# A fused attention, mixer and feed-forward kernel: weight conversion moved between slots, a rounding moved from VectorE to ScalarE, and folds put in another order

## The chip, the cores and the metric

One core of a Trainium2 chip runs the whole program. The metric is the device time of one execution in microseconds; before and after are each given as the median of several executions, and one more execution is run under the profiler.

## The reference, cut to what is computed

```python
attn = A @ Z @ C @ v                      # landmark attention per head, Z by six Newton steps
x1 = moe(attn):   u = x + (x^T U V)^T;    x1 = u + relu(u @ w11) @ w12
X = np.fft.fft(np.fft.fft(x1, axis=1), axis=2)
u = x1 + np.real(X)
mu = np.mean(u, axis=-1, keepdims=True)
var = np.mean((u - mu) ** 2, axis=-1, keepdims=True)
un = (u - mu) / np.sqrt(var + 1e-06)
out = u + np.maximum(un @ w21, 0.0) @ w22
```

There are 8 batches of 576 tokens with 512 features; the hidden width of both feed-forward parts is 2048. The inputs are float32 and the weights float64.

## The kernel before, in words

Every operand of a matmul is held as two parts, a high part rounded to the matmul's format (fp32r) and a low part that holds the rest. A product of two such pairs takes three matmuls. The helper `split` (L49) makes a pair: ScalarE copies the value into the high part (L51), and VectorE or GpSimd subtracts it to get the low part (L52).

The float64 weights are converted on the chip. One piece (128 rows by 512 values) passes through `convert` (L90): `TENSOR_SCALAR`, `SCALAR_TENSOR_TENSOR`, `TENSOR_SCALAR`, `SCALAR_TENSOR_TENSOR`, `TENSOR_TENSOR` and one more `SCALAR_TENSOR_TENSOR` on VectorE (L96 to L106), an absolute value on ScalarE (L101), and the split into the tile `stg` on ScalarE and GpSimd. The result goes to DRAM with a DMA of 512 KB. There is one `stg` buffer, so the next split waits until that DMA has landed, and two buffers `wraw` for the float64 pieces.

The feed-forward work is a stream of slots. A slot is 12 matmuls of 128x512. In a first-layer slot, `up` (L318) then takes the bank from PSUM: ScalarE makes the high part with a Relu (L329), VectorE the low part (L330). There are 3 banks for it. In a second-layer slot pair, VectorE adds the former sum (L387), or ScalarE copies the bank (L385). The stage that matters here is the loop at L1582: 144 slots of the second pass and 96 of the third. Into it are laid, slot by slot, the instructions of eight `Mixer` objects (L1139), one for each batch, which compute the Fourier mixing and the normalisation. A mixer starts every 25 slots, from slot 33 on (L1577). Its list `steps` (L1339) is a table of numbers: (slot, step). The order in which a slot is written is: the stream's instructions, then the mixers' steps, then the conversion. All engines work their instructions in that order.

The mixer's steps that matter:

- `fold_d`, `fold_t`, `fold_2` (L1171 to L1186): VectorE folds the batch's data into an even part "e" and an odd part "o". `fold_split` (L1187) copies the high part on ScalarE (`he`, `ho`), `fold_low` (L1193) subtracts the low part on VectorE (`le`, `lo`). `over_d` (L1219) multiplies them with a table, from slot 10 of the mixer (even) and 13 (odd) on.
- `sums` (L1288), called by `sum_u` and `sum_sq` for each half n of the tokens, adds the four blocks of 128 features. It makes a pair in the tiles `he`, `ho`, `le`, `lo` again (four VectorE instructions, L1291 to L1294). `mean` (L1296) multiplies the pair with a matrix of 1/512. `centre` (L1305) subtracts the mean, ScalarE squares the result (L1314), `deviation` (L1317) calls `mean` a second time.
- The conversion runs as a generator. `Pace.step(n)` (L1468) takes up to n of its pieces in a slot; at the end of a weight piece it stops until the next slot. `BUSY` (L1580) names the mixer's slots in which nothing is converted.

```python
later = Pace(chained([staging_pairs(cv, 2), staging_sums(cv), staging_blocks(cv)]))
BUSY = (0, 1, *range(4, 9), 21, 22)
later.step(0 if s > 33 and (s - 33) % 25 in BUSY else 2)
```

Slot numbers of 25 and more of one mixer are the slots 0, 1, 2 and so on of the next one. In what follows the mixers are counted from the first to the eighth.

Of the kernel before, what the change touches and what calls it, by code (L numbers as in the profile page):

```python
# [15 lines left out]
ALU = mybir.AluOpType  # L16
# [18 lines left out]
def f32(ap):  # L35
    return ap.bitcast(F32)
# [3 lines left out]
def body(ctx: ExitStack, tc: tile.TileContext, qT, kT, vn, mU, mV, w11, w12, w21, w22,  # L40
         ident, bones, istack, tabs, out):
    nc = tc.nc
# [1096 lines left out]
    class Mixer:  # L1139
# [148 lines left out]
        def sums(self, n, x, nm):  # L1288
            a = self.fp.tile([P, 2, 290], F32, name="cc", bufs=2)[:, :, 0:HS]
            s = self.half[n]["s"] = self.fp.tile([P, 2, NF], F32R, name=nm + "eo"[n], bufs=1)[:, :, 0:HS]  # L1290
            nc.vector.tensor_tensor(a, x[:, 0:2], x[:, 2:4], op=ALU.add)  # L1291
            nc.vector.tensor_tensor(s[:, 0, :], a[:, 0, :], a[:, 1, :], op=ALU.add)
            nc.vector.tensor_tensor(a[:, 0, :], a[:, 0, :], f32(s[:, 0, :]), op=ALU.subtract)
            nc.vector.tensor_tensor(s[:, 1, :], a[:, 0, :], a[:, 1, :], op=ALU.add)  # L1294

        def mean(self, n):  # L1296
            ps = self.bank("l")[:, 0:HS]
# [39 lines left out]
            nc.sync.dma_start(rs[self.b][:, self.cols(n)], self.half[n]["r"])  # L1337

        def steps(self):  # L1339
            yield from ((0, self.load), (2, self.load_first), (3, self.fold_x), (4, self.sum_row), (5, self.row_high), (5, lambda: self.fold_d("e")),  # L1340
                        (5, lambda: self.fold_t("e")), (6, lambda: self.fold_d("o")), (6, lambda: self.fold_2("e")),
                        (7, self.fold_row), (7, lambda: self.fold_t("o")), (8, lambda: self.fold_split("e")),
                        (8, self.row_low), (8, lambda: self.fold_2("o")), (9, lambda: self.fold_low("e")),
                        (9, lambda: self.fold_split("o")), (10, lambda: self.fold_low("o")),
                        (11, self.load_rows))
            yield from ((s, lambda nm=nm, i=i: self.over_d(nm, i)) for s, nm, i in
                        ((10, "e", 0), (11, "e", 1), (12, "e", 2), (13, "o", 0), (14, "o", 1), (14, "o", 2)))
            yield from ((15, self.top_row), (16, lambda: self.odd(0)), (17, lambda: self.even(0)),
                        (18, lambda: self.unfold(0)), (18, lambda: self.unfold(3)), (18, lambda: self.odd(1)),
                        (19, lambda: self.even(1)), (20, lambda: self.unfold(1)), (20, lambda: self.unfold(2)),  # L1350
                        (21, self.store))
            for n in range(2):
                yield from ((21 + n, lambda n=n: self.sum_u(n)), (24 + n, lambda n=n: self.centre(n)),
                            (25 + n, lambda n=n: self.sum_sq(n)), (28 + n, lambda n=n: self.deviation(n)),
                            (26 + n, lambda n=n: self.put(n)), (29 + n, lambda n=n: self.newton(n)),
                            (30 + n, lambda n=n: self.put_scale(n)))

# [122 lines left out]
    with pool("mm") as mp, pool("pm", space=PSUM) as pm:  # L1480
# [91 lines left out]
        with tc.manual_schedule(), pool("cv") as cv:  # L1572
            with pool("fp") as fp, pool("fc") as fc, pool("pf", space=PSUM) as psb:
                f = {}
                slots = Slots()
                for b in range(B):
                    slots.add(33 + 25 * b, Mixer(fp, psb, f, b).steps())  # L1577
                later = Pace(chained([staging_pairs(cv, 2), staging_sums(cv), staging_blocks(cv)]))
                gen = mlp.stream(1)
                BUSY = (0, 1, *range(4, 9), 21, 22)  # L1580
                setup = fourier_setup(f, fc, fp)
                for s in range(N + 96):  # L1582
                    if s == N:
                        some(gen, 9)
                        gen = mlp.stream(2)
                    next(gen)
                    slots.run(s)
                    next(setup, 0)
                    later.step(0 if s > 33 and (s - 33) % 25 in BUSY else 2)
            assert not slots.at  # L1590
            chunks = [(0,)] + [(c, c + 1) for c in range(1, NCH, 2)]
            kinds = [(chunks[-1:], None, ByChunk(y2), quarter[0], None),
                     (chunks[-1:], ByChunk(y2), ByChunk(y2), quarter[1], None),
                     (chunks, ByChunk(y2), ByChunk(y3), staged[3][0:11], None),
                     (chunks, ByChunk(y3), Y, staged[3][11:22], (Scales(rs), U2))]
            with pool("tl") as mlp.last_pool, pool("tp", space=PSUM) as mlp.last_ps:
                last = mlp.quarters(UN, kinds, lambda s: s % 2 and later.step(2))
                next(last)
                for s in range(STEPS):
                    next(gen)  # L1600
                    next(last)
                    later.step(0 if s > 6 else 1)
                some(gen, 9)
                for _ in last:
                    pass
                later.rest()
# [83 lines left out]
```

## Time and profile before

| | |
|---|---|
| median of 3 runs | 1818.57 us (1816.17 to 1820.9) |
| profiled execution, its own time | 1816.94 us |
| its span, first to last instruction | 1815.2 us |
| TensorE matmul (PE) busy | 1786.8 us, 98% |
| VectorE (DVE) busy | 1117.6 us, 62% |
| ScalarE (ACT) busy | 734.9 us, 40% |
| GpSimd (POOL) busy | 274.5 us, 15% |
| DMA, mean rate | 182 GB/s |
| mean granted TensorE clock | 0.998 |

The busy share of an engine is an average over stages. The end of a matmul in the trace is modelled, so that a busy TensorE says little; the views that tell of the stage are the waits of TensorE, the chain of work that ended last and the instructions in order of time.

### The profile page before, as it was taken

Reading aid. Unit: us, or ns where it says so; the run is one execution under the profiler, and the core shown is the slowest. Engines: PE = TensorE matmul, PEld = TensorE weight load, DVE = VectorE, ACT = ScalarE, POOL = GpSimd, SP = SyncE. Lnnn points to the kernel's source line nnn. Section 1 sums busy time; section 2 is a strip of 40 time slices with the busy share of each in tenths; the row PEclk is TensorE's granted clock in tenths of the full one; section 3 lists DMA queues with packets and bytes.
Section 4 is the critical chain, followed back from the end, with each engine's and each line's share of the span. In section 5 each row is a group of like instructions: output and inputs, shape, how many; then the busy total and the mean of one; then the engine's idle time right before and its main releaser. Section 6 shows DMA issues by size and latency. Waiting matters only on the chain.

```text
span 1815.2 us, 30889 instructions
## 1 busy us (share of the span) xinstructions
PE 1786.8 (98%) x12037; PEld 1456.7 (80%) x12037; DVE 1117.6 (62%) x1984; ACT 734.9 (40%) x1507; POOL 274.5 (15%) x278
## 2 busy tenths in 40 slices
PE   6999999999999999999999999999999999999998
PEld 4777777777888888888888888888788888888887
DVE  7896665665423666847666685756651465438874
ACT  4554444344212333323233243434333566545542
POOL 3324221221200321111112111111200000000000
PEclk9999999999999999999999999999999999999999
DMA  7555456542448654535445753424466745477765
GB/s 250 184 174 179 148 168 212 170 153 100 142 146 292 206 199 163 190 115 192 143 163 194 274 178 119 141 105 151 157 208 223 275 157 167 146 256 244 225 192 162
DMA packets 189238, 329.57 MB, mean 182 GB/s; under 512 B 28938, under 2 KB 101226, under 8 KB 189092
## 3 DMA queue, kind: packets, MB, share of 16 engines
q1 hardware_dynamic: 184484, 318.16, 52.5%
q10 hardware_dynamic: 4608, 9.44, 1.4%
q8 instruction: 94, 1.54, 0.3%
q14 instruction: 52, 0.43, 0.1%
HBM read 213.42 MB, written 113.51 MB: 180 GB/s over the span
## 4 chain that ended last, share of the span: by engine, by line
PE 85%; DVE 9%; DMA 2%; ACT 2%; issue 1%; POOL 0%; SPq 0%; DVEq 0%; ACTq 0%
PE ps L377 9%; PE ps L379 8%; PE ps L378 8%; PE ps L325 8%; PE ps L327 8%; PE ps L326 8%; PE ps L593 4%; PE ps L594 4%; PE ps L592 4%; PE ps L417 4%; PE ps L416 4%; PE ps L418 4%; PE ps_f L77 1%; PE ps_f L78 1%; PE ps_f L76 1%
## 5 line engine op out<-in xcount | busy, mean ns | idle before, releaser
L325 PE MATMUL ps<-x,w 128*128 128x512 f32 x800 | 317.8, 397 | 0.0
L377 PE MATMUL ps<-g,w 128*128 128x512 f32 x800 | 316.6, 396 | 0.0
L379 PE MATMUL ps<-g,w 128*128 128x512 f32 x800 | 312.1, 390 | 0.1
L327 PE MATMUL ps<-x,w 128*128 128x512 f32 x800 | 312.1, 390 | 0.0
L326 PE MATMUL ps<-x,w 128*128 128x512 f32 x800 | 311.8, 390 | 0.0
L378 PE MATMUL ps<-g,w 128*128 128x512 f32 x800 | 311.6, 390 | 0.0
L330 DVE SCALAR_TENSOR_TENSOR g<-ps,g 128x512 fp32r<-128x512 f32 x200 | 137.8, 689 | 234.0 <-ACT g L329 233.5
L329 ACT ACTIVATE g<-ps 128x512 fp32r<-128x512 f32 x200 | 119.0, 596 | 312.7 <-PE ps L327 312.2
L377 PEld LDWEIGHTS ps<-g,w 128*128 128x128 f32 x800 | 150.2, 188 | 33.3 <-issue 3.5
L379 PEld LDWEIGHTS ps<-g,w 128*128 128x128 f32 x800 | 150.1, 188 | 32.7 <-DVE g L330 0.5
L327 PEld LDWEIGHTS ps<-x,w 128*128 128x128 f32 x800 | 150.2, 188 | 32.5
L325 PEld LDWEIGHTS ps<-x,w 128*128 128x128 f32 x800 | 150.2, 188 | 30.5
L378 PEld LDWEIGHTS ps<-g,w 128*128 128x128 f32 x800 | 150.4, 188 | 28.5
L326 PEld LDWEIGHTS ps<-x,w 128*128 128x128 f32 x800 | 150.5, 188 | 28.2
L592 PE MATMUL ps<-g,w 128*128 128x512 f32 x352 | 136.9, 389 | 0.0
L593 PE MATMUL ps<-g,w 128*128 128x512 f32 x352 | 136.9, 389 | 0.0
L594 PE MATMUL ps<-g,w 128*128 128x512 f32 x352 | 136.9, 389 | 0.0
L387 DVE TENSOR_TENSOR xf<-ps,xf 128x512 f32<-128x512 f32 x76 | 52.2, 687 | 86.7 <-PE ps L379 85.0
L52 POOL TENSOR_TENSOR x<-xf,x 128x512 fp32r<-128x512 f32 (+7 forms) x50 | 62.5, 1252 | 206.6 <-ACT x L51 183.5
L416 PE MATMUL ps<-xs,w 128*128 128x512 f32 x208 | 80.9, 389 | 0.0
L417 PE MATMUL ps<-xs,w 128*128 128x512 f32 x208 | 80.9, 389 | 0.0
L418 PE MATMUL ps<-xs,w 128*128 128x512 f32 x208 | 80.9, 389 | 0.0
(388 smaller groups left out, 2999.5 us busy)
## 6 DMA issues: line engine op xcount, KB each, us to landing
w<-d SPq DMA_DIRECT2D x62, 512.0 KB
d<-stg SPq DMA_DIRECT2D x54, 512.0 KB
wraw<-w SPq DMA_DIRECT2D x48, 512.0 KB
res<-y SPq DMA_DIRECT2D x80, 256.0 KB
y<-xf SPq DMA_DIRECT2D x64, 256.0 KB
y<-out SPq DMA_DIRECT2D x52, 256.0 KB
xf<-y SPq DMA_DIRECT2D x40, 256.0 KB
u<-u1T ACTq DMA_DIRECT2D x32, 288.0 KB
```

The source lines that it names most:

```text
L325: nc.tensor.matmul(ps, wh, xh, start=k == 0, stop=False)
L326: nc.tensor.matmul(ps, wl, xh, start=False, stop=False)
L327: nc.tensor.matmul(ps, wh, xl, start=False, stop=k == 3)
L377: nc.tensor.matmul(ps, wh, gh, start=k == m0, stop=False)
L378: nc.tensor.matmul(ps, wl, gh, start=False, stop=False)
L379: nc.tensor.matmul(ps, wh, gl, start=False, stop=k == m1 - 1)
L416: nc.tensor.matmul(ps, wh, xh, start=first and k == 0, stop=False, skip_group_check=True)
L417: nc.tensor.matmul(ps, wl, xh, start=False, stop=False, skip_group_check=True)
L418: nc.tensor.matmul(ps, wh, xl, start=False, stop=last and k == 1, skip_group_check=True)
L592: nc.tensor.matmul(ps[j], wh, gh, start=first, stop=False, skip_group_check=True)
L593: nc.tensor.matmul(ps[j], wl, gh, start=False, stop=False, skip_group_check=True)
L594: nc.tensor.matmul(ps[j], wh, gl, start=False, stop=k == ks[3], skip_group_check=True)
```

## The change

Three things change. First, `sums` no longer writes the high part with an add. It adds the blocks in full float32, ScalarE copies (and so rounds) the result, and the low part is one subtraction in a new step `sums_low`, one slot after `sum_u` and two slots after `sum_sq`. Second, the folds are given other slots: the even part goes through to its low part at mixer slot 8 (it was 9), and the odd folds follow. Third, the conversion has no part in mixer slots 2 and 3 either, and in the slots that are left takes up to 3 pieces (it was 2); in the last stage it takes up to 2 in the first seven slots (it was 1).

```diff
             nc.vector.tensor_tensor(a, x[:, 0:2], x[:, 2:4], op=ALU.add)
-            nc.vector.tensor_tensor(s[:, 0, :], a[:, 0, :], a[:, 1, :], op=ALU.add)
-            nc.vector.tensor_tensor(a[:, 0, :], a[:, 0, :], f32(s[:, 0, :]), op=ALU.subtract)
-            nc.vector.tensor_tensor(s[:, 1, :], a[:, 0, :], a[:, 1, :], op=ALU.add)
+            nc.vector.tensor_tensor(a[:, 0, :], a[:, 0, :], a[:, 1, :], op=ALU.add)
+            self.half[n]["a"] = a[:, 0, :]
+            nc.scalar.copy(s[:, 0, :], a[:, 0, :])
+
+        def sums_low(self, n):
+            a, s = self.half[n]["a"], self.half[n]["s"]
+            nc.vector.tensor_tensor(s[:, 1, :], a, f32(s[:, 0, :]), op=ALU.subtract)
...
-                        (8, self.row_low), (8, lambda: self.fold_2("o")), (9, lambda: self.fold_low("e")),
+                        (8, lambda: self.fold_low("e")), (8, lambda: self.fold_t("o")),
...
-                yield from ((21 + n, lambda n=n: self.sum_u(n)), (24 + n, lambda n=n: self.centre(n)),
-                            (25 + n, lambda n=n: self.sum_sq(n)), (28 + n, lambda n=n: self.deviation(n)),
+                yield from ((21 + n, lambda n=n: self.sum_u(n)), (22 + n, lambda n=n: self.sums_low(n)), (24 + n, lambda n=n: self.centre(n)),
+                            (25 + n, lambda n=n: self.sum_sq(n)), (27 + n, lambda n=n: self.sums_low(n)), (28 + n, lambda n=n: self.deviation(n)),
...
-                BUSY = (0, 1, *range(4, 9), 21, 22)
+                BUSY = (*range(0, 9), 21, 22)
...
-                    later.step(0 if s > 33 and (s - 33) % 25 in BUSY else 2)
+                    later.step(0 if s > 33 and (s - 33) % 25 in BUSY else 3)
...
-                    later.step(0 if s > 6 else 1)
+                    later.step(0 if s > 6 else 2)
```

TensorE's instructions and their order are the same before and after. Three places where the order on the other engines differs:

VectorE, the folds of the third mixer, before (`big` holds a fold that is being made, `cc` its second step, `le` and `he` the even low and high parts):

```order
L1175 TENSOR_TENSOR big<-U 128x1152
L1179 TENSOR_TENSOR big<-big 128x2x287
L387 TENSOR_TENSOR xf<-ps,xf 128x512
L1175 TENSOR_TENSOR big<-U 128x1152
L1185 TENSOR_TENSOR cc<-big 128x289 x2
L52 TENSOR_TENSOR x<-xf,x 128x512
L1208 TENSOR_TENSOR cc<-X 1x289
L1179 TENSOR_TENSOR big<-big 128x2x287
L387 TENSOR_TENSOR xf<-ps,xf 128x512
L1216 TENSOR_TENSOR X<-X,row 1x289
L1185 TENSOR_TENSOR cc<-big 128x289 x2
L1195 TENSOR_TENSOR le<-cc,he 128x578
```

and now:

```order
L1175 TENSOR_TENSOR big<-U 128x1152
L1179 TENSOR_TENSOR big<-big 128x2x287
L387 TENSOR_TENSOR xf<-ps,xf 128x512
L1185 TENSOR_TENSOR cc<-big 128x289 x2
L1208 TENSOR_TENSOR cc<-X 1x289
L1216 TENSOR_TENSOR X<-X,row 1x289
L52 TENSOR_TENSOR x<-xf,x 128x512
L1175 TENSOR_TENSOR big<-U 128x1152
L387 TENSOR_TENSOR xf<-ps,xf 128x512
L1195 TENSOR_TENSOR le<-cc,he 128x578
L1179 TENSOR_TENSOR big<-big 128x2x287
L1185 TENSOR_TENSOR cc<-big 128x289 x2
```

The second and third odd folds now stand behind the even low part, not ahead of it.

VectorE, the sums of squares of the fourth mixer, before, from the first `centre` on (`Z<-U,ps_l`); `le` and `lo` are the pairs of the first and second half, and `g<-ps,g` is the stream's low part of a slot:

```order
L1309 TENSOR_TENSOR Z<-U,ps_l 128x1152
L330 SCALAR_TENSOR_TENSOR g<-ps,g 128x512
L1291 TENSOR_TENSOR cc<-big 128x2x288
L1292 TENSOR_TENSOR le<-cc 128x288
L1293 TENSOR_TENSOR cc<-cc,le 128x288
L1294 TENSOR_TENSOR le<-cc 128x288
L1309 TENSOR_TENSOR Z<-U,ps_l 128x1152
L330 SCALAR_TENSOR_TENSOR g<-ps,g 128x512
L1291 TENSOR_TENSOR cc<-big 128x2x288
L1292 TENSOR_TENSOR lo<-cc 128x288
L1293 TENSOR_TENSOR cc<-cc,lo 128x288
L1294 TENSOR_TENSOR lo<-cc 128x288
```

and now, from the last two conversion instructions on (three more stand ahead of them, behind the first `centre`; before, this place held none):

```order
L134 SCALAR_TENSOR_TENSOR cvp<-wraw,cvp 128x512
L135 TENSOR_TENSOR cvp<-cvp,cva 128x512
L330 SCALAR_TENSOR_TENSOR g<-ps,g 128x512
L1291 TENSOR_TENSOR cc<-big 128x2x288
L1292 TENSOR_TENSOR cc<-cc 128x288
L1313 TENSOR_TENSOR Z<-U,ps_l 128x1152
L330 SCALAR_TENSOR_TENSOR g<-ps,g 128x512
L1291 TENSOR_TENSOR cc<-big 128x2x288
L1292 TENSOR_TENSOR cc<-cc 128x288
L330 SCALAR_TENSOR_TENSOR g<-ps,g 128x512
L1298 TENSOR_TENSOR le<-cc,le 128x288
```

The pair of the first half, `le`, was complete ahead of the second `centre`; now it is complete only behind the second half's sums and behind the stream's low part of one more slot.

ScalarE at the same place, before (`big<-Z` is the square):

```order
L329 ACTIVATE g<-ps 128x512
L1314 ACTIVATE big<-Z 128x1152
L329 ACTIVATE g<-ps 128x512
L1314 ACTIVATE big<-Z 128x1152
L329 ACTIVATE g<-ps 128x512
L51 CAST x<-xf 128x512
```

and now:

```order
L132 ACTIVATE wraw<-wraw 128x512
L329 ACTIVATE g<-ps 128x512
L1318 ACTIVATE big<-Z 128x1152
L1294 CAST le<-cc 128x288
L329 ACTIVATE g<-ps 128x512
L1318 ACTIVATE big<-Z 128x1152
L1294 CAST lo<-cc 128x288
L329 ACTIVATE g<-ps 128x512
L51 CAST x<-xf 128x512
```

A copy of each half's high part now stands behind its square and ahead of the stream's next Relu.

## Rows read from the trace of the kernel before

**Rows 1.** Windows: stretch, length, then busy time (and count) by engine.

```profile
582.00:690.00 108.00, 108.00 (x478) 89.41 (x477) 76.41 (x116) 35.27 (x62) 28.56 (x23) 1.00 0.58 194
690.00:1310.00 620.00, 614.91 (x3043) 516.25 (x3042) 416.02 (x698) 212.50 (x407) 102.42 (x88) 1.00 0.48 164
1350.00:1790.00 440.00, 440.00 (x1943) 364.34 (x1942) 245.36 (x387) 235.74 (x427) 0.00 (x0) 1.00 0.64 204
```

**Rows 2.** Waits of TensorE, 650 to 1330 us: total us, times, longest.

```profile
PE ps_l L1299 <- DVE lo L1294: 2.0, 2, 1.5
PE ps_f L77 <- DVE le L1195: 1.7, 2, 0.9
PE ps_f L1250 <- DVE Z L52: 1.2, 1, 1.2
```

**Rows 3.** Timeline of VectorE, folds of the third mixer (start us, us).

```profile
846.47 0.74 DVE L1179 TENSOR_TENSOR big<-big 128x574 f32<-128x574 f32 x1
848.11 0.81 DVE L1185 TENSOR_TENSOR cc<-big 128x289 f32<-128x289 f32 x2
848.85 0.74 DVE L1195 TENSOR_TENSOR le<-cc,he 128x578 fp32r<-128x578 f32 x1
```

**Rows 4.** Timeline of TensorE, the same place.

```profile
848.52 0.23 PE L76 MATMUL ps_f<-tabl,he 128*97 128x146 f32 x1
849.64 0.31 PE L77 MATMUL ps_f<-tabh,le 128*97 128x146 f32 x1 [0.90 <-DVE le L1195]
```

**Rows 5.** Timeline of VectorE, second half's sums of the eighth mixer.

```profile
1307.50 1.41 DVE L1293 TENSOR_TENSOR cc<-cc,lo 128x288 f32<-128x288 f32 x1
```

**Rows 6.** Timeline of VectorE, sums of squares of the second mixer.

```profile
822.38 0.76 DVE L1291 TENSOR_TENSOR cc<-big 128x576 f32<-128x576 f32 x1 [0.37 <-ACT big L1314]
823.17 0.46 DVE L1292 TENSOR_TENSOR le<-cc 128x288 fp32r<-128x288 f32 x1
...
824.53 1.35 DVE L1309 TENSOR_TENSOR Z<-U,ps_l 128x1152 f32<-128x1152 f32 x1
825.80 0.68 DVE L330 SCALAR_TENSOR_TENSOR g<-ps,g 128x512 fp32r<-128x512 f32 x1
827.12 0.76 DVE L1291 TENSOR_TENSOR cc<-big 128x576 f32<-128x576 f32 x1 [0.64 <-ACT big L1314]
```

**Rows 7.** Timeline of ScalarE, the same place.

```profile
823.68 0.60 ACT L329 ACTIVATE g<-ps 128x512 fp32r<-128x512 f32 x1 [1.34 <-PE ps L327]
825.91 1.17 ACT L1314 ACTIVATE big<-Z 128x1152 f32<-128x1152 f32 x1 [1.64 <-DVE Z L1309]
826.99 0.58 ACT L329 ACTIVATE g<-ps 128x512 fp32r<-128x512 f32 x1
```

**Rows 8.** Timeline of TensorE, second mean of the first half, second mixer.

```profile
828.92 0.42 PE L1299 MATMUL ps_l<-le,ones 128*128 128x288 f32 x2
```

**Rows 9.** Groups by line, ScalarE, 690 to 1310 us: an instruction of 128x288.

```profile
L1324 ACT ACTIVATE r<-r 128x288 f32<-128x288 f32 x14 | 6.2, 443 | 0.0
```

**Rows 10.** Timeline of VectorE: first of a piece's six conversion instructions, and what follows them.

```profile
1285.10 0.41 DVE L96 TENSOR_SCALAR cva<-wraw 128x512 uint32<-128x512 uint32 x1
...
1288.87 0.68 DVE L330 SCALAR_TENSOR_TENSOR g<-ps,g 128x512 fp32r<-128x512 f32 x1
```

**Rows 11.** Timeline of ScalarE, fourth mixer, the Relu ahead of the first centre.

```profile
976.89 0.60 ACT L329 ACTIVATE g<-ps 128x512 fp32r<-128x512 f32 x1 [1.55 <-PE ps L327]
```

**Rows 12.** Timeline of TensorE, fourth mixer, second mean of the first half.

```profile
988.13 0.42 PE L1299 MATMUL ps_l<-le,ones 128*128 128x288 f32 x2
```

**Rows 13.** Chain that ended last, 994 to 1030 us, fifth mixer.

```profile
1016.08 7.85 DMA d<-stg
1024.03 0.62 ACT stg L51
```

**Rows 14.** Waits of ScalarE, 455 to 700 us.

```profile
ACT stg L51 <- DMA xf<-u: 2.7, 1, 2.7
```

**Rows 15.** Timeline of ScalarE: a converted piece is split.

```profile
590.25 0.62 ACT L51 CAST stg<-cva 128x512 fp32r<-128x512 f32 x1 [1.94 <-DVE cva L106]
```

**Rows 16.** Timeline of the DMA queue: the same piece is stored.

```profile
592.26 0.33 SPq L1413 DMA_DIRECT2D d<-stg  x1
```

More of the change, by code (lines that the diff above doesn't have):

```diff
@@ L1339, in steps @@
         def steps(self):
-            yield from ((0, self.load), (2, self.load_first), (3, self.fold_x), (4, self.sum_row), (5, self.row_high), (5, lambda: self.fold_d("e")),
-                        (5, lambda: self.fold_t("e")), (6, lambda: self.fold_d("o")), (6, lambda: self.fold_2("e")),
-                        (7, self.fold_row), (7, lambda: self.fold_t("o")), (8, lambda: self.fold_split("e")),
-                        (8, self.row_low), (8, lambda: self.fold_2("o")), (9, lambda: self.fold_low("e")),
-                        (9, lambda: self.fold_split("o")), (10, lambda: self.fold_low("o")),
-                        (11, self.load_rows))
+            yield from ((0, self.load), (2, self.load_first), (3, self.fold_x), (4, self.sum_row), (5, self.row_high),
+                        (5, lambda: self.fold_d("e")), (5, lambda: self.fold_t("e")), (6, lambda: self.fold_2("e")),
+                        (6, self.fold_row), (6, self.row_low), (7, lambda: self.fold_split("e")), (7, lambda: self.fold_d("o")),
+                        (8, lambda: self.fold_low("e")), (8, lambda: self.fold_t("o")),
+                        (9, lambda: self.fold_2("o")), (9, lambda: self.fold_split("o")),
+                        (10, lambda: self.fold_low("o")), (11, self.load_rows))
             yield from ((s, lambda nm=nm, i=i: self.over_d(nm, i)) for s, nm, i in
```

## The prediction

> **What bounds the kernel now.** I read the windows first [rows 1]. In the stretch with the mixers (690 to 1310 us) TensorE is busy for 614.9 of 620 us, so all that better timing of the other engines can give back there is about 5 us. Before it (582 to 690 us) and behind it (1350 to 1790 us) TensorE is never idle. TensorE's own work does not change, so the whole case is a sum of waits of TensorE that go and waits that come.
>
> Here a rule speaks for more room. Matmul ends are modelled, and by the Trainium skill ("Perfetto Trace Analysis", Identifying the Most-Contended Engine) busy matmul time is a poor measure of how near the ceiling is; weight-load time is the better one. Weight loads fill 516 of 620 us, and by that rule some 100 us would be left. The rows decide against it: in the tail, where TensorE waits for nothing, the share is the same, 364 of 440 us, 83%. I go on with 5 us.
>
> The waits of TensorE [rows 2] name the places: 2.0 us for the low part of the second half's sum of squares (`lo`), 1.7 us for the even fold's low part (`le`, L77), 1.2 us once for a PSUM bank that a split had not yet left (L1250). Together 4.9 us. Counted from start to start they are somewhat longer: 848.52 to 849.64 for matmuls that otherwise follow within 0.1 us is 1.0 and not 0.9 us [rows 4]. I put them at 2.4, 2.0 and 1.3 us, 5.7 in all.
>
> **The folds.** In the third mixer `le` began at 848.85 and TensorE waited for it [rows 3, 4]. The change takes one odd `L1179` (0.7 us) and a pair of `L1185` (0.8 us) from ahead of it, 1.5 us; the wait was 1.0. No conversion precedes it in slots 2 and 3 either. The odd part, which falls back, is needed three slots later. These waits go: **-2.0 us** (bounds -1.7 and -2.2).
>
> **The low part of the second half.** The longer of the two waits was 1.5 us in the eighth mixer [rows 2]; there one subtraction of 0.46 us took 1.41 [rows 5], and a piece of conversion stood ahead. Now two instructions of 0.46 us fewer stand in each half's sums, and the last subtraction has until slot 29. In the first and eighth mixer I find 0.5 us or more to spare: **-2.4 us** (bounds -2.5 and, if a stretched instruction falls there again, -1).
>
> **The low part of the first half is what is late next.** This is where the change adds a wait. Before, VectorE completed `le` ahead of the second centre. Now the subtraction comes two slots later, behind the stream's low part (L330); that waits for ScalarE's Relu (L329); and the Relu stands behind ScalarE's new copy for the second half, which waits for that half's sums. I follow it in the second mixer. VectorE starts the sum at 822.38; the next instruction follows 0.79 later [rows 6], an add of 0.46 ends at 823.63, and the second centre, no longer behind two more instructions, starts there. ScalarE's square starts 1.38 us behind the centre's start (824.53 to 825.91) [rows 6, 7], at 825.0. The second half's sum starts 1.21 us after that, at 826.2, and with 0.79 and 0.46 ends at 827.5. The copy takes 0.44 [rows 9], the Relu 0.60 [rows 7], L330 0.68, the subtraction 0.46, and at a hand-over of some 0.05 each `le` is ready at 829.7. TensorE reaches its pair of matmuls at 828.92 [rows 8], and the one with the low part 0.13 later, at 829.05. It would wait 0.6 us, where before it had about 4 us to spare.
>
> In the fourth mixer five of the six conversion instructions now stand behind the first centre. Six take 3.77 us [rows 10], five 3.1. From the Relu at 976.89 [rows 11]: 0.6 and 0.65 to the end of L330, 1.27 for the centre (824.53 to 825.80), 3.1 of conversion to 982.5, 0.6 for L330, 0.79 and 0.46 for the sum to 984.4, 1.27 for the second centre to 985.6; then 1.2, 0.79 and 0.46 bring the second sum to 988.2, and copy, Relu, L330 and subtraction (2.2) bring `le` to 990.4. TensorE wants it at 988.13 plus 0.13 [rows 12]: 2.1 us. The fifth and seventh mixers have a conversion at the same slot and Relus behind it, and lie between the two; I take 1.0 each. In the first, third, sixth and eighth the stream is in its second layer, no Relu stands between, and 0.5 us or more is left. Sum **+4.7 us** (bounds 0, if the copy never gets ahead of the Relu, and 8, if every mixer loses 1 us).
>
> **The bank wait.** In the fifth mixer ScalarE sat until a store of 7.85 us had landed, since the next split needs the one `stg` buffer [rows 13]; Z's split queued behind it. The same two splits stand in the same two slots after the change: **0** (bounds -1.3 and +2, as the queue has one more or less of these transfers ahead).
>
> **The first stretch.** Ahead of the mixers one weight piece every three slots becomes one every two. A slot is 12 matmuls at 108 us for 478 [rows 1], 2.7 us, so the period falls from 8.1 to 5.4. VectorE's load is 3.8 us for a piece and 1.3 for two slots of the stream, 5.1 of 5.4: it fits, barely. The store goes out 2.0 us after the split starts [rows 15, 16] and has 3.4 us to land where it had 6.1. A store took 7.85 us with the queue full [rows 13], and before only one of the splits here waited for a transfer, 2.7 us [rows 14]. ScalarE's and VectorE's lag reaches TensorE only beyond about 2.4 us, as three banks give two slots (5.4 us) for Relu, L330 and the piece's instructions. I expect one or two such moments: **+1.0 us** (bounds 0 and +8). Nearest is the lower one, from the single wait on record.
>
> **The rest.** ScalarE's 32 copies at 0.44 us lie beside its idle time (busy for a third of the mixers' stretch, 212 of 620 us). Without that cover they would cost what I counted above, as nothing else queues behind them that TensorE needs soon. Fewer pieces of conversion fall late, so the last stage starts with about as much left to convert: 0.
>
> Sum: -2.0 - 2.4 + 4.7 + 0 + 1.0 = +1.3 us on the profiled 1816.94 us. That run is 1.6 us below the median of 1818.57; on the median the sum gives **1819.9 us**. I count 0.3% (5.5 us) as what a measurement can tell from no change.
>
> **The rivals.**
>
> *Every wait goes and none comes.* VectorE is relieved of 32 instructions of 0.46 us, and were the copies always in time, the 4.7 us would not arise; with the first stretch calm the time is 1818.6 - 5.7, about 1813 us. For it: ScalarE is two-thirds idle. The Trainium skill has the rule that favours it ("Perfetto Trace Analysis", Optimizing Scalar/DVE Operations): work that a busy VectorE hands to ScalarE, and instructions broken up where they make other engines wait, may be done sooner; by that rule the time would be these 1813 us. Against it stands the in-order queue that I followed above: what counts is not ScalarE's load but what stands behind the copy. Chance 0.18, and about half of that beyond 0.3%.
>
> *The first stretch turns to waiting: slower.* The loop there is split, store, landing, next split. Once a landing takes more than 3.4 us, each piece comes later than its two slots; at a landing of 4 us 0.6 us is lost with each of the 14 pieces, 8.4 us less the 2.4 us that the banks cover, +6 us, and with the other terms 1825.9. It decides from a mean landing of 3.6 us on. For it: the DMA engines are already 58% busy there [rows 1] and get half as many pieces more. Against it: only one wait for a transfer on record. Chance 0.17.
>
> *The change only trades places.* That is the forecast: the sums' waits move from `lo` to `le`, the folds' wait goes. Chance 0.60. The remaining 0.05 is for something not seen, either side.
>
> **How the numbers follow.** Faster by over 0.3%: 0.09 of the first rival and a little of the rest, 0.10. Slower: the second rival and a part of the upper bounds, 0.20. Within 0.3%: 0.70. The range goes from 1814.0 (all waits gone but a small one) to 1826.0 (the slow rival at its price).
>
> **What would show it.** In the profile after, the waits of TensorE should have no `le` at the fold matmuls and little or no `lo` at the means, but `le` at the means in the second, fourth, fifth and seventh mixers, 0.5 to 2 us each. On ScalarE a copy should stand ahead of a late Relu there. The L1250 wait should be much as it was. From 582 to 690 us TensorE should be idle for 1 us or less. The forecast is wrong if `le` at the means does not appear (then about 1815) or if TensorE idles for more than 5 us ahead of the mixers.

## The result, and the profile after

| | before | after |
|---|---|---|
| median of the runs | 1818.57 us (1816.17 to 1820.9) | 1835.33 us (1833.35 to 1836.9) |
| span of the profiled execution | 1815.2 us | 1833.5 us |
| mean granted TensorE clock | 0.998 | 0.997 |

The ratio of after to before is 1.0092, with a 95% interval of 1.0078 to 1.0107: the change makes the kernel slower by 16.8 us. The forecast was 1819.9 us; the time lies above its range of 1814.0 to 1826.0 us.

The stretch ahead of the mixers in the changed kernel (its window, length, busy time and count of TensorE, of its weight loads, VectorE, ScalarE and GpSimd, then the granted clock, DMA share and GB/s):

```profile
582.00:690.00 108.00, 98.45 (x412) 78.58 (x411) 82.88 (x123) 34.69 (x59) 30.79 (x25) 0.97 0.65 223
```

Between 582 and 690 us TensorE ran 478 matmuls before [rows 1] and now 412. At 108 us for 478 a matmul is 0.226 us, so 66 fewer are **14.9 us lost ahead of the mixers**. The kernels that wait for nothing in this stretch have 478 to 483 matmuls there, so such a count is good to about 1 us. From 1350 to 1790 us nothing is lost: TensorE is busy for 440.00 us with 1943 matmuls, as before. The waits of TensorE, 450 to 1335 us, say for what it waited:

```profile
PE ps L325 <- DVE xf L387: 7.6, 4, 2.9
PE ps_l L1303 <- DVE le L1298: 7.1, 7, 1.7
PE ps_f L76 <- DVE Z L52: 1.1, 1, 1.1
PE ps L379 <- DVE g L330: 0.9, 1, 0.9
PE ps L377 <- DVE g L330: 0.6, 1, 0.6
PE ps L325 <- DVE g L330: 0.5, 2, 0.2
```

Two rows are the mixers': 8.2 us, where [rows 2] had 4.9, so the mixers lose 3.3 us more than before. (A line number is that of the kernel that ran: the changed kernel's L1298 is the subtraction of `sums_low`, L1294 its copy on ScalarE, L1303 the matmul of `mean`, which is L1299 before.) The other four lie ahead of the mixers, 9.6 us. Three of them are PSUM banks that VectorE has not yet emptied, 8.7 us; at L379 it is a low part `g` that VectorE has not yet made, 0.9 us. The two losses, 14.9 and 3.3, make 18.2 us; the spans differ by 18.3.

Why is VectorE late ahead of the mixers? Its timeline there (start, duration, in brackets the idle time ahead and what ended it), first around the end of a chunk of the stream, then in the stream's first layer:

```profile
609.62 1.59 DVE L106 SCALAR_TENSOR_TENSOR cva<-wraw,cvp 128x512 f32<-128x512 f32 x1
611.14 0.68 DVE L387 TENSOR_TENSOR xf<-ps,xf 128x512 f32<-128x512 f32 x1
613.64 0.77 DVE L96 TENSOR_SCALAR cva<-wraw 128x512 uint32<-128x512 uint32 x1 [1.82 <-POOL stg L52]
...
617.75 0.68 DVE L387 TENSOR_TENSOR xf<-ps,xf 128x512 f32<-128x512 f32 x1
619.93 0.76 DVE L96 TENSOR_SCALAR cva<-wraw 128x512 uint32<-128x512 uint32 x1 [1.50 <-POOL stg L52]
...
626.23 0.43 DVE L96 TENSOR_SCALAR cva<-wraw 128x512 uint32<-128x512 uint32 x1 [0.19 <-POOL stg L52]
...
629.40 0.69 DVE L106 SCALAR_TENSOR_TENSOR cva<-wraw,cvp 128x512 f32<-128x512 f32 x1
630.01 0.68 DVE L330 SCALAR_TENSOR_TENSOR g<-ps,g 128x512 fp32r<-128x512 f32 x1
631.32 0.69 DVE L330 SCALAR_TENSOR_TENSOR g<-ps,g 128x512 fp32r<-128x512 f32 x1 [0.63 <-ACT g L329]
632.20 0.43 DVE L96 TENSOR_SCALAR cva<-wraw 128x512 uint32<-128x512 uint32 x1 [0.18 <-POOL stg L52]
```

L96 is the first instruction of a piece of weights. From one L96 to the next are 6.29 us (613.64 to 619.93) and 5.97 us (626.23 to 632.20), and a piece has two slots, 5.42 us (24 matmuls at 0.226). Between L106 of one piece and L96 of the next VectorE waits each time: for GpSimd, which still reads the one buffer of converted words (`cva`), or for ScalarE, mostly for its Relu. That Relu is late since it stands behind the split of the piece, which itself had to wait for VectorE's L106; ScalarE's timeline:

```profile
630.17 0.62 ACT L51 CAST stg<-cva 128x512 fp32r<-128x512 f32 x1 [1.59 <-DVE cva L106]
630.70 0.59 ACT L329 ACTIVATE g<-ps 128x512 fp32r<-128x512 f32 x1
```

The stream's additions L387 stand in VectorE's queue behind these waits, and TensorE's banks with them. The busy time is not small either. From the first to the last of the 15 L96 in the stretch (585.12 to 677.38) VectorE is busy for 74.35 us, 5.31 for each of 14 pieces: besides the piece and the stream it makes low parts of `x` there (L52, four times 1.36 us), and five of the 15 L106 take 1.59 to 1.72 us where the others take 0.69.

Which of the waits decides the pace is the first question for the experiments; the second is what the mixers' part of the change is worth by itself.

### The profile page after: what moved, and what is told of

It is laid out like the page before. It is cut to its first block, busy times and chain, and to the rows that moved or that the text cites. A ratio compares the mean times of both kernels' runs of the same rounds, so it can differ in the third digit from the quotient of the medians.

```text
span 1833.5 us, 30906 instructions
## 1 busy us (share of the span) xinstructions
PE 1791.1 (98%) x12037; PEld 1457.3 (79%) x12037; DVE 1107.1 (60%) x1952; ACT 747.5 (41%) x1539; POOL 274.7 (15%) x278
## 5 line engine op out<-in xcount | busy, mean ns | idle before, releaser
L379 PE MATMUL ps<-g,w 128*128 128x512 f32 x800 | 312.2, 390 | 0.9 <-DVE g L330 0.9
L330 DVE SCALAR_TENSOR_TENSOR g<-ps,g 128x512 fp32r<-128x512 f32 x200 | 137.9, 689 | 247.6 <-ACT g L329 246.9
L379 PEld LDWEIGHTS ps<-g,w 128*128 128x128 f32 x800 | 150.1, 188 | 33.6 <-DVE g L330 1.3
L387 DVE TENSOR_TENSOR xf<-ps,xf 128x512 f32<-128x512 f32 x76 | 52.2, 687 | 89.3 <-PE ps L379 87.6
L52 POOL TENSOR_TENSOR x<-xf,x 128x512 fp32r<-128x512 f32 (+7 forms) x50 | 65.5, 1312 | 220.5 <-ACT x L51 197.4
```

The source lines that it names most:

```text
L379: nc.tensor.matmul(ps, wh, gl, start=False, stop=k == m1 - 1)
```

## The experiments

All were timed in five rounds beside the kernel before (whose medians there are 1817.85 to 1818.25 us), except the two with L104 left out (three rounds). A weight piece needs three slots at two steps a slot and two slots at three. The table names the parts of the change each one has: the folds' order, the sums, the conversion's slots in the mixers with three steps a slot behind slot 33 and two in the last stage (slots), and three steps up to slot 33 (early). "Lost early" is (478 - matmuls from 582 to 690 us) x 0.226 us, "mixers' waits" the sum of TensorE's waits from 690 to 1335 us.

| run | parts | median, us | ratio, 95% interval | lost early | mixers' waits |
|---|---|---|---|---|---|
| before | none | 1818.57 | 1 | 0 | 4.9 |
| after | all | 1835.33 | 1.0078 to 1.0107 | 14.9 | 8.2 |
| e1 | folds, sums, slots | 1814.68 | 0.9973 to 0.9991 | 0 | 3.0 |
| e2 | early | 1827.36 | 1.0037 to 1.0062 | 14.9 | 2.3 |
| e3 | all, two buffers | 1832.73 | 1.0066 to 1.0091 | 13.3 | 7.1 |
| e4 | folds, slots, early | 1828.22 | 1.0043 to 1.0070 | 14.0 | 3.0 |
| e5 | folds, slots | **1810.87** | 0.9946 to 0.9972 | 0 | 0.4 |
| e6 | folds | 1816.06 | 0.9981 to 0.9998 | 0 | 4.4 |
| e7 | sums | 1828.45 | 1.0040 to 1.0069 | 0 | 12.7 |
| e8 | all, two buffers, no L104 | 1823.01 | 1.0017 to 1.0037 | 3.2 | 7.4 |
| e9 | slots | 1811.62 | 0.9950 to 0.9975 | 0 | 1.6 |
| e10 | folds, slots, sums with `le` earlier | 1811.53 | 0.9947 to 0.9975 | 0 | 1.2 |
| e11 | all, one buffer, no L104 | 1823.73 | 1.0017 to 1.0040 | 2.9 | 7.6 |
| e12 | sums with `le` earlier | 1820.10 | 1.0005 to 1.0023 | 0 | 6.0 |

### Where the 14.9 us are lost

**e1: the change without its pace in the first stretch.**

```diff
-                    later.step(0 if s > 33 and (s - 33) % 25 in BUSY else 3)
+                    later.step(0 if s > 33 and (s - 33) % 25 in BUSY else 3 if s > 33 else 2)
```

> The changed kernel with two conversion steps a slot instead of three up to slot 33, three behind it. Theory A (the first stretch, at three steps a slot, turns round a loop over the single converted-words buffer that is longer than two slots): the 14.9 us that TensorE loses between 582 and 690 us go, TensorE idles there for at most 1 us, the granted clock stays at 1.00, and the run takes 1820 us (1818 to 1823). Rival (the mixers' part of the change costs more than their waits show): 1826 us or more, with TensorE as full as before up to 690 us.

Measured: 1814.68 us. The 14.9 us are gone and, beyond what was expected, the rest of the change is faster than before. The time is below the expected 1818 to 1823 us. Its waits of TensorE, 450 to 1335 us, are one row:

```profile
PE ps_l L1303 <- DVE le L1298: 3.0, 4, 1.7
```

**e2: that pace alone, on the kernel before** (its `later.step` with `2 if s > 33 else 3`).

> The kernel before with three conversion steps a slot instead of two up to slot 33 and nothing else changed. Theory A: the first stretch alone loses 15 us, 1832 us (1829 to 1836), with the same waits of TensorE for the stream's addition L387 and the two drops of the granted clock. Rival (the reordered mixers feed back on the first stretch, or only the whole change shows it): 1818 to 1823 us. The prediction's own rival (the loop through the store's landing, 0.6 us a piece): 1824 us.

Measured: 1827.36 us. The waits for L387 are the same to the digit (7.6, 4, 2.9), and the first of these windows has the same 412 matmuls:

```profile
582.00:690.00 108.00, 98.68 (x412) 78.70 (x411) 85.53 (x128) 34.59 (x59) 30.84 (x25) 0.97 0.65 222
690.00:1310.00 620.00, 617.42 (x3058) 519.16 (x3057) 408.04 (x683) 210.96 (x407) 98.17 (x85) 1.00 0.46 159
```

The time is 5 us below the 1832 expected and below the theory's range. The second row gives some 3 us of that: the mixers have 15 matmuls more than in [rows 1], and the waits there fall from 4.9 to 2.3 us. The rest is not traced. So the 14.9 us belong to the pace in the first stretch alone; no part of the mixers has a hand in them.

**e3: two buffers of converted words.**

```diff
-    def convert(cv, raw, out, bufs=1):
+    def convert(cv, raw, out, bufs=1, nm="cva"):
...
-        a = cv.tile([P, 512], U32, name="cva", bufs=2 * bufs - 1)
+        a = cv.tile([P, 512], U32, name=nm, bufs=2 * bufs - 1)
...
-            for _ in convert(cv, raws[i], st, 1):
+            for _ in convert(cv, raws[i], st, 1, "cva" if i % 2 else "blk"):
```

> The changed kernel, with the paired pieces' converted words alternating between two buffers (the second one is the blocks' tile, idle at that time), so that the next piece's first instruction on VectorE no longer waits for GpSimd's subtraction of the piece before; stores, fetches, the staged tile and VectorE's load are as they were. Theory A: 1821 to 1827 us; the waits for L387 in 582 to 690 us fall from 7.6 us to below 2 us and the drops of the clock go. Rival B (the staged tile's store must land before the next split): 1832 to 1835 us, with the wait standing at the split on ScalarE and TensorE's waits as they were. Rival C (VectorE's load in two slots): 1833 to 1836 us, VectorE without a wait there and TensorE's waits as they were.

Measured: 1832.73 us, a miss for the theory that I held first. In VectorE's own waits, 582 to 690 us, the changed kernel has

```profile
DVE g L330 <- ACT g L329: 11.2, 11, 2.0
DVE cva L96 <- POOL stg L52: 7.2, 9, 1.8
...
DVE cva L96 <- DMA wraw<-w: 0.3, 1, 0.3
```

and with two buffers

```profile
DVE g L330 <- ACT g L329: 14.1, 12, 2.2
...
DVE cva L96 <- DMA wraw<-w: 2.2, 2, 1.1
```

The 7.2 us for GpSimd are gone, and 4.8 of them have come back as waits for ScalarE (2.9) and for the fetch (1.9). From the first to the last of 15 L96 in the stretch a piece takes 6.36 us on average (585.18 to 674.26) where it took 6.59 (585.12 to 677.38), still far over 5.42. TensorE still waits 7.0 us for L387, and the granted clock, which was to stay up, is 0.95 in the stretch. The one buffer was only the first of several things that fill the same gap.

**e8 and e11: one instruction less for VectorE in each piece**, with two buffers and with one. L104, one of VectorE's six instructions (0.69 us), is left out of the paired pieces; the third pass then works with other weights.

```diff
-        (nc.gpsimd if bufs > 1 else nc.vector).tensor_tensor(pf, pf, af, op=ALU.add)
+        if not light:
+            (nc.gpsimd if bufs > 1 else nc.vector).tensor_tensor(pf, pf, af, op=ALU.add)
```

> The changed kernel with two buffers for the converted words (as in the run with two buffers) and with VectorE's addition L104 left out of the paired pieces, so that VectorE has 0.72 us less to do in each piece; the third pass's weights are wrong by it, nothing else moves. Theory after the run with two buffers (VectorE itself is the bound of the first stretch: 3.8 us of conversion, two stream instructions of 0.69 and one wait of 0.63 for ScalarE make 5.9 to 6.0 us in two slots of 5.44): 5.2 us fit, TensorE's waits in 582 to 690 us fall from 7.4 to below 1.5 us, the clock stays up, 1818 to 1822 us. Rival B (the staged tile's store, or the fetch, sets the pace): 1829 us or more, TensorE's waits above 5 us as in the run with two buffers.

> The changed kernel with VectorE's addition L104 left out of the paired pieces, so that the third pass's weights are wrong, and with the one buffer for the converted words. Theory (VectorE's whole time for a piece decides, the one buffer only as far as it fills that time): as with two buffers and the same left out, 1821 to 1825 us, and TensorE loses 3 to 5 us in 582 to 690 us. Rival (the loop over the single buffer has a length of its own, which the left-out instruction shortens too little): 1828 us or more.

Measured: 1823.01 and 1823.73 us, 9.7 and 11.6 us below the same kernels with L104 (e3 and the changed kernel). e8 is 1 us above its theory's range, e11 within it. The stretch in e8:

```profile
582.00:690.00 108.00, 106.07 (x464) 86.25 (x463) 77.01 (x118) 38.89 (x67) 30.85 (x26) 1.00 0.68 229
```

TensorE loses 3.2 us there (2.9 in e11), and the clock's share is back at 1.00. One buffer or two makes no difference any more: a piece takes 5.84 us on average in both (584.52 to 666.29 and 585.03 to 666.81, 15 L96 each). So what decides is **how long VectorE's whole round for a piece is**: six instructions, those of the stream, and the hand-overs at which it must stand. Leaving out L104 takes 0.97 us of busy time out of a round in both pairs (5.46 to 4.49 and 5.31 to 4.34), 0.69 its own and the rest mainly because L106 no longer meets a subtraction on GpSimd (it takes 0.69 us in all 15 pieces). It gives back 10.1 us of TensorE's time (e8 against e3) or 12.0 (e11 against the change); the one wait out of the round gave back 1.6.

A part of the rest can be read on ScalarE in e8 (whose lines behind L104 are one higher; L330 is the Relu here):

```profile
630.48 0.62 ACT L51 CAST stg<-cva 128x512 fp32r<-128x512 f32 x1 [2.40 <-DMA d<-stg]
631.01 0.59 ACT L330 ACTIVATE g<-ps 128x512 fp32r<-128x512 f32 x1
...
636.24 0.63 ACT L51 CAST stg<-blk 128x512 fp32r<-128x512 f32 x1 [1.55 <-DMA d<-stg]
```

The split waits for the store of the piece before, and the stream's Relu stands behind the split. That is the loop that the prediction's slow rival named; here its round is 5.76 us (630.48 to 636.24). In e8 five of 15 splits wait for a store, and four of 15 L96 for the fetch of their piece (5.6 us). These are the next limits, and they did not set the 6.59 us: in the changed kernel three of 15 splits wait for a store, 0.2 to 0.6 us beyond the L106 they need anyway, and one L96 for a fetch (0.3 us).

### What the mixers' part is worth

**e4: the change with the old sums**, and **e5: the same with two steps up to slot 33** (e1's edit). In both, `sums` is as before and `sums_low` goes.

> The changed kernel with the sums as before (high part written by VectorE's own addition, low part by two more VectorE instructions in the same slot), so that ScalarE's copy and the later step go; pace and fold order stay changed. Theory: the seven waits for the low part at the second mean (7.1 us) go, the waits for the second half's low part (2.0 us before) come back: 1835.3 - 7.1 + 2.0 = 1830 us (1828 to 1832). Rival (the copy and the late low part only trade places with the old waits, and the loss is the first stretch's alone): 1834 to 1836 us.

> The changed kernel with both the sums as before and two conversion steps a slot up to slot 33; what is left of the change is the fold order and the conversion's slots behind slot 33. Theory (sums' copy costs 3.0 us of waits for the low part at the second mean at this pace and takes away 2.0 us for the second half's low part): 1813 to 1815 us, equal to the 1814.7 us of the run with the new sums within 1.5 us, with waits for the second half's low part of about 2 us back and none for the first half's. Rival (the sums' copy is what costs, as the 7 us between the changed kernel and the one with old sums suggest): 1808 to 1811 us.

Measured: 1828.22 us, 7.1 less than with the new sums and within the range expected, and 1810.87 us, 3.8 less than e1. For e5 that is 2 us below what the theory gave, and in its rival's range: the waits for the second half's `lo`, which were to come back with the old sums, stay away (0.4 us, and 0.7 in e4). So it is not the sums that had removed them. e5 has the lowest median of the study, 0.9959 of before (0.9946 to 0.9972); e9 and e10 cannot be told from it. In its mixers TensorE waits 0.4 us in all; the window of the mixers:

```profile
690.00:1310.00 620.00, 619.65 (x3070) 521.88 (x3069) 416.46 (x688) 215.33 (x414) 104.46 (x88) 1.00 0.47 161
```

Next to nothing is left to win there by order: busy for 619.65 of 620 us, with weight loads at 84%.

**e6, e7, e9: the folds, the sums and the slots, each alone on the kernel before.**

```diff
-                BUSY = (0, 1, *range(4, 9), 21, 22)
+                BUSY = (*range(0, 9), 21, 22)
...
-                    later.step(0 if s > 33 and (s - 33) % 25 in BUSY else 2)
+                    later.step(0 if s > 33 and (s - 33) % 25 in BUSY else 3 if s > 33 else 2)
...
-                    later.step(0 if s > 6 else 1)
+                    later.step(0 if s > 6 else 2)
```

(That is e9; e6 has the change's first list of `steps`, up to `load_rows`, e7 its `sums`, `sums_low` and the list in which they stand.)

> The kernel before with the fold order alone changed. The prediction's term: the waits for the even fold's low part (1.7 us) go, 2.0 us less than before, 1816 us (1815 to 1817.5). Rival (the odd folds or the first product's tables become late instead): 1818 us, no change, with waits at the fold's products of the odd half.

> The kernel before with the sums alone changed (addition in fp32, copy on ScalarE, low part a slot later). The prediction's terms: -2.4 us for the second half's low part and +4.7 us for the first half's at the second mean, 1820.3 us (1817 to 1822). Rival (the wait depends on which conversion step falls in the slot of the low part, and is as often there as with the change): 1823 to 1825 us, waits for the first half's low part of 7 us. Rival (GpSimd and ScalarE take the copy beside the rest): 1815 to 1817 us, no such wait.

> The kernel before with the conversion's slots alone changed, and that only behind slot 33: nothing in the mixers' slots 2 and 3, three steps instead of two in the light ones, two up to slot 33 as before. Theory (the slots are what gains: the run with old sums at this pace is 7.0 us below before, the fold order alone 1.8): 1811 to 1814 us, waits for the second half's low part and for the first product's bank (2.0 and 1.2 us before) below 1 us in all. Rival (only fold order and slots together gain, the fold waits stand in the lightened slots): 1815 us or more, the fold's 1.7 us of waits as before.

Measured: 1816.06, 1828.45 and 1811.62 us. By their ratios the folds give 1.8 us (0.4 to 3.5), the slots 6.9 (4.5 to 9.1). In the two traces the slots' gain is 5.0 us of the span (1815.2 to 1810.2), all but 0.1 of it ahead of 1360 us. The slots do what the prediction had credited to the sums: in e9's waits of TensorE, 0.4 us of the second half's `lo` is left, and L1250 is gone.

```profile
PE ps_f L77 <- DVE le L1195: 1.2, 1, 1.2
PE ps_l L1299 <- DVE lo L1294: 0.4, 1, 0.4
```

The sums alone cost 9.8 us, more than any of the expectations. TensorE's waits in e7, 690 to 1335 us:

```profile
PE ps_l L1303 <- DVE le L1298: 7.9, 5, 2.5
PE ps_l L1303 <- DVE lo L1298: 2.3, 1, 2.3
PE ps_f L77 <- DVE le L1195: 1.7, 1, 1.7
PE ps_l L1303 <- DVE ho L1298: 0.8, 1, 0.8
```

These are 7.8 us more than before, and behind two of them the granted clock fell (0.60 from 1157 to 1160 us, 0.59 from 1319 to 1322). The reason of the waits stands in VectorE's queue. In e7's first mixer ScalarE's copy for `le` was done at 749.25 (748.82 plus 0.43), and VectorE reached the subtraction 3.2 us later (the copy on ScalarE, then VectorE's timeline):

```profile
748.82 0.43 ACT L1294 CAST le<-cc 128x288 fp32r<-128x288 f32 x1 [1.42 <-DVE cc L1292]
```

```profile
748.70 1.35 DVE L1313 TENSOR_TENSOR Z<-U,ps_l 128x1152 f32<-128x1152 f32 x1
749.97 0.68 DVE L387 TENSOR_TENSOR xf<-ps,xf 128x512 f32<-128x512 f32 x1
751.29 0.76 DVE L1291 TENSOR_TENSOR cc<-big 128x576 f32<-128x576 f32 x1 [0.64 <-ACT big L1318]
752.08 0.46 DVE L1292 TENSOR_TENSOR cc<-cc 128x288 f32<-128x288 f32 x1
752.46 0.45 DVE L1298 TENSOR_TENSOR le<-cc,le 128x288 fp32r<-128x288 f32 x1
```

`le` waits here behind the second half's centre and sums, and the sums wait for ScalarE's square. Neither the copy nor a Relu delays it in this mixer.

**e10 and e12: `le` one slot earlier**, ahead of the second half's sums, with ScalarE's copy kept (on e1 and on e7).

```diff
-                            (25 + n, lambda n=n: self.sum_sq(n)), (27 + n, lambda n=n: self.sums_low(n)), (28 + n, lambda n=n: self.deviation(n)),
+                            (25 + n, lambda n=n: self.sum_sq(n)), (26 + 2 * n, lambda n=n: self.sums_low(n)), (28 + n, lambda n=n: self.deviation(n)),
```

> The changed kernel at two steps a slot up to slot 33, with the first half's second low part one slot earlier, ahead of the second half's sums on VectorE; ScalarE's copy stays. Theory (the low part is late because VectorE reaches it behind the second half's sums, which wait for ScalarE's squares): the 3.0 us of waits for the first half's low part go, 1811 to 1812.5 us, level with the old sums' 1810.9. Rival (the copy on ScalarE is late or stands ahead of the stream's Relu): 1814 to 1816 us, with waits at the same mean or at the stream's matmuls.

> The kernel before with the sums alone changed, as in the run with the sums alone, but the first half's second low part stands one slot earlier, ahead of the second half's sums. Theory (the copy costs nothing, only the low part's place does): the 7.9 us of waits for the first half's low part fall below 1.5 us, no drop of the granted clock, 1816 to 1820 us. Rival (at the pace of before, the copy or the second half's chain is late whatever the place): 1823 us or more, the waits now at the second half's parts.

Measured: 1811.53 us, 3.2 less than e1 and level with the old sums, and 1820.10 us, 8.3 less than e7. In e10 no wait for `le` is left; there VectorE makes it at 981.94, with the second half's first sum at 982.66 behind it (VectorE's timeline, fourth mixer):

```profile
981.34 0.68 DVE L330 SCALAR_TENSOR_TENSOR g<-ps,g 128x512 fp32r<-128x512 f32 x1
981.94 0.45 DVE L1298 TENSOR_TENSOR le<-cc,le 128x288 fp32r<-128x288 f32 x1
982.66 0.76 DVE L1291 TENSOR_TENSOR cc<-big 128x576 f32<-128x576 f32 x1 [0.27 <-ACT big L1318]
```

e12 is just outside its expectation of 1816 to 1820: 1.2 us for `le` remain, and 3.0 for the second half's parts. The longest of these, 2.2 us for `lo` in the sixth mixer, is the place of a low part again: the copy was done at 1148.51, and VectorE reached the subtraction at 1152.53, behind five conversion instructions and a split of the stream. So the copy on ScalarE is not what costs, but it gains nothing either; the place of the low parts is the price.

## Why the prediction was wrong

**The first stretch, forecast +1.0 us with bounds of 0 and +8, measured 14.9.** This is the step that failed: "VectorE's load is 3.8 us for a piece and 1.3 for two slots of the stream, 5.1 of 5.4: it fits, barely." Two terms were mis-sized. The load itself was 5.31 us, not 5.1, since the low parts of `x` and the slow L106 were left out. And the waits, put at nothing, were 1.28 us a round: a load that leaves 0.1 us in 5.42 does not fit when the engine works in order and has to stand at hand-overs. In this stretch each round had at least one: in the stream's first layer the Relu for the second L330 stands on ScalarE behind the split that waits for VectorE (0.63 us at 631.32), at a chunk's end a low part of `x` waits for its copy on ScalarE (0.65 us), and GpSimd's hold on `cva` (0.18 to 1.82 us) comes on top. The round was 6.59 us on average, 1.17 more than two slots; over 14 rounds that is 16 us, of which the banks took up a part. In the kernel before VectorE also waited for GpSimd's subtraction in this stretch, once:

```profile
DVE cva L96 <- POOL stg L52: 1.2, 1, 1.2
```

With three slots a piece that cost nothing, and I left it out.

**The slow rival** had the right place and sign, but the wrong loop and too low a price: +6 us by the store's landing, deciding from 3.6 us on. e3, e8 and e11 show that VectorE's round decides; the store and the fetch come behind it, where 3 us are lost. Its time of 1825.9 us also counts the stretch twice, since the 1819.9 that it adds 6 us to has the +1.0 in it. Its chance of 0.17 was for a special loop, while the plain load stood in the text as the thing that fits.

**The folds, forecast -2.0:** alone -1.8 us (0.9981 to 0.9998). The sign agrees, but that the size does is luck within this interval: one of the two waits stayed in e6 (L77, 0.9 us), and its trace has 0.5 us less of waits in all. Both waits are gone only together with the slots (e5).

**`lo`, forecast -2.4 by two VectorE instructions fewer:** the waits did go in the change, but by the slots. With the sums alone they stayed (2.3 us for `lo` in e7); with the slots alone 0.4 us is left.

**`le`, forecast +4.7 in the second, fourth, fifth and seventh mixers:** mechanism right, too few mixers. In the change these four wait 4.0 us together, near the forecast, but the third, sixth and eighth, where I saw 0.5 us to spare, wait another 3.1. The fourth mixer of the change has the chain as I followed it: the second half's copy, the Relu behind it, L330 waiting for that Relu, then the subtraction (ScalarE, then VectorE).

```profile
1003.79 0.43 ACT L1294 CAST lo<-cc 128x288 fp32r<-128x288 f32 x1 [1.32 <-DVE cc L1292]
1004.13 0.59 ACT L329 ACTIVATE g<-ps 128x512 fp32r<-128x512 f32 x1
```

```profile
1004.75 0.69 DVE L330 SCALAR_TENSOR_TENSOR g<-ps,g 128x512 fp32r<-128x512 f32 x1 [1.00 <-ACT g L329]
1005.36 0.45 DVE L1298 TENSOR_TENSOR le<-cc,le 128x288 fp32r<-128x288 f32 x1
```

In e1, whose first stretch runs as before, it was 3.0 us in the second, fourth, sixth and seventh; for the fourth I had 2.1, and the wait is 1.67 (TensorE):

```profile
986.99 0.40 PE L1303 MATMUL ps_l<-le,ones 128*128 128x288 f32 x1 [1.67 <-DVE le L1298]
```

What was too narrow is the condition that a Relu must stand between: the first mixer of e7 has none, only L387, and TensorE waits there too (VectorE made `le` at 752.46, above). The second half's sums, with their wait for the square, are delay enough. Where a conversion piece falls may then shift it by a us or two; no run tests that by itself. The same edit cost 3.8 us at one pace (e1 against e5), 7.1 at another (after against e4) and 9.8 on the kernel before.

**The bank wait, forecast 0 with a bound of -1.3:** L1250 is gone in e9 and in the change, the lower bound; the change has another one of 1.1 us (L76), so that its net is near the forecast.

**What was not in the sum at all** is the conversion's slots as a gain. In the mixers "the rest" was put at 0, and the slots alone are worth 6.9 us by the ratio and 5.0 by the spans. The bound of about 5 us for all that timing can give back in the mixers was nearly right: e5 has 27 more matmuls there than before, 5.5 us, with 0.4 us of waits left. Its whole gain is 7.5 us by the ratio (5.1 to 9.8) and 7.2 by the spans; where the rest of it comes from is not traced.

**The rule of the Trainium skill that spoke for a gain** ("Perfetto Trace Analysis", Optimizing Scalar/DVE Operations) says that handing work to ScalarE may make sense where VectorE is saturated, and that breaking up instructions may let work be done sooner where these engines are not saturated but hold up others. VectorE was busy for 416 of 620 us in the mixers [rows 1], so the first condition is hardly met. The second way brought no gain here: with the copy on ScalarE the kernel is 9.8 us slower (e7), and with the low part better placed 2.5 us slower (e12) or as fast as without it (e10 against e5).

Left open: which hand-over in VectorE's round is the costliest, since they stand in for one another, and whether a split written behind the Relu would shorten it; and whether the last 3 us of the first stretch go with a second `stg` buffer, which was not tried.

## What to carry to other kernels

When a change packs more work into the same slots, compare the slot with the in-order engine's whole round, hand-overs included, and not with its busy time: waits that cost nothing at three slots a piece made the round 1.17 us too long at two. If the round is too long, taking one wait away only moves it to the next one; take instructions out or lower the pace. And when an instruction is split in two, ask what the in-order queue puts between the halves: here the second half's sums, worth 3 to 8 us of waits, and one slot earlier 0 to 1.2.

## What the hardware showed that was not expected

The granted clock fell to half its level inside the first stretch of the changed kernel. TensorE's timeline and two windows (the clock is the third value from the end):

```profile
618.49 0.50 PE L325 MATMUL ps<-x,w 128*128 128x512 f32 x1 [2.01 <-DVE xf L387]
...
619.08 0.63 PE L327 MATMUL ps<-x,w 128*128 128x512 f32 x1
```

```profile
619.00:622.00 3.00, 3.00 (x8) 2.33 (x8) 1.97 (x4) 0.55 (x1) 1.77 (x4) 0.50 0.67 249
677.20:680.40 3.20, 3.20 (x9) 2.46 (x9) 2.88 (x5) 1.16 (x2) 0.15 (x1) 0.50 0.89 296
```

0.5 is the level of 1.2 GHz. Matmuls 0.226 us apart are 0.43 apart from 619.08 to 622.07 and again from 677.31 to 680.30, seven each time: 14 by 0.2 are some 2.8 us of the 14.9. With the 9.6 us of waits that makes 12.4; no row names the other 2.5. TensorE had been idle for 2.0 us ahead of the first fall and for 2.9 ahead of the second. A wait of 2.2 us in e12, which ended at 1153.6 us, was followed by a clock of 1.00, so the length of one wait does not tell by itself. So an idle TensorE can cost more than the idle time.

VectorE's L106 took 1.59 us instead of 0.69 at 609.62, while GpSimd subtracted beside it (608.90 to 610.67, 1.77 us where the subtraction for `stg`, of the same size, takes 1.29 by itself). L106 ended at 611.21, 0.54 us behind GpSimd's instruction, as if it had stood until that was nearly through. The same stands in all five slow L106 of the stretch: each meets an instruction of GpSimd and ends 0.54 or 0.55 us behind it. No run tests it by itself. The Trainium skill ("SBUF — State Buffer", SBUF: two separate sides) has a rule that fits: VectorE, in an instruction with two inputs from SBUF (as L106 has), and GpSimd share a pair of ports, and of two such instructions the one that starts first holds the pair to its end while the other stands. The trace agrees in the order of events; that L106 ends 0.54 us behind the other, where it needs 0.69 by itself, the rule does not explain.
